# Value products in four 64x64 quarters of the array, keys in chunks of 64 per head, and a new plan, in an attention and token-mixing kernel

## The chip, the cores and the metric

The kernel runs on one core of one Trainium2 chip, in one launch. The metric is the device time of the whole program in microseconds (us). Everything is in 32-bit floats; matrix products of full precision are built on TensorE either from pairs of rounded parts (`float32r`) or from plain `float32` operands.

## The reference, cut to what matters

`q`, `k` and `v` are 8 batches x 8 heads x 576 positions x 64 numbers. The scores are scaled, all scores below the row's maximum minus `tau` are masked, and a softmax follows. The heads of a batch are laid side by side and give `x` (8 x 576 x 512), which goes through a mixture over channels and tokens.

```python
scores = scale * np.matmul(q, k.transpose(0, 1, 3, 2))
thresh = np.max(scores, axis=-1, keepdims=True) - tau
scores = np.where(scores >= thresh, scores, -1000000000.0)
attn = np.exp(scores - np.max(scores, axis=-1, keepdims=True))
attn = attn / (np.sum(attn, axis=-1, keepdims=True) + 1e-09)
x = np.matmul(attn, v)
...
theta = x @ w_theta
y = einsum('ts,bsd->btd', w_tok_r, x * cos(theta)) + einsum('ts,bsd->btd', w_tok_i, x * sin(theta))
u = x + y
out = u + np.maximum(u @ w_ch, 0.0)
```

## The kernel before, in words

The work is cut into 32 pairs of heads (`n`), four to a batch. For each pair, `attention` (L997) loads and splits `q` and `k` (`prepare_q` L500, `prepare_k` L512), loads `v` (`load_v` L520), runs five units, two groups of value products, and a division. After the four pairs of a batch the `mixture` (L758) of that batch follows; its steps are mixed in time with the attention of the next batch.

A **unit** (L535) is a block of 128 queries of both heads (`i` from 0 to 3), or the last 64 queries of both heads in one block (`i` = 4). It has these steps. The score products (L552) go into PSUM banks 0 to 3: for `i` < 4 two products at a time, each on 64 rows of the array (one head each), 12 matmuls of 288 columns. In the first five pairs (`n < AT["pp"]`, with `pp` = 5) VectorE reduces both heads' scores to the negated maximum (L567), ScalarE takes the exponential straight from PSUM (L614), and VectorE masks straight from PSUM and sums (L621). In the other pairs VectorE first copies the negated scores to SBUF and finds the maximum in the same instruction (L583), ScalarE (L631) and VectorE (L638) work from the copy. `nm` holds the thresholds (L592 or L600). TensorE then transposes the weights in blocks of 128x128 (L654, L681), and ScalarE copies them from PSUM into `a0` or `a1` (L660, L668, L686, L694). In the last unit ScalarE first copies 64 columns (L674).

The **value products** (`values`, L698, matmuls at L710) are made twice per pair: group 0 for the first 256 queries, group 1 for the other 320. Each has, for both heads, five chunks of 128 keys; the fifth holds 64 keys of each head, and the other half of its weights are zeros (`v5`). The stationary operand is 128 rows x 64 columns, so one head's product uses the left 64 columns of the array and the other head's the right 64, both into one PSUM bank, one in the upper and one in the lower 64 partitions. Operands are plain `float32`, and the trace shows two MATMUL and two LDWEIGHTS instructions for each product: 20 per group. ScalarE copies the result to `xT` (L717).

`divide` (L721) turns the row sums into reciprocals on VectorE (L734), writes them to DRAM, reads them back spread over the partitions (three DMAs, L737) and multiplies (L745).

`convert` (L377) makes the two `float32r` parts of the 64-bit weights: four chunks of `w_theta` and nine of `w_tok` at the start, four of `w_ch` in the first mixture. Each chunk costs five VectorE instructions (L411, L418, L425, L432, L436), ScalarE instructions (L407, L447, L461) and three products (L455 to L457).

The order on every engine is written by a planner, `Plan.run` (L147): it simulates the five engines with a cost per step and puts first, of the steps that could start within `AT["wait"]` of the earliest, the one with the smallest key. Keys count 9 per pair, plus the offsets in `AT` (L33). `bank()` (L322) gives PSUM banks 7 to 2, or only 7 to 4 for steps of the first pairs. All DMAs go through the SP queue.

Of the kernel before, what the change touches and what calls it, by code (L numbers as in the profile page):

```python
# [32 lines left out]
AT = {  # L33
    "wait": 0.046, "margin": 0.0, "held": 1.639, "theta": 3.43, "theta_by": 2.2, "tok": 17.5, "tok_by": 0.87, "ch": 54.39,
    "ch_by": 3.55, "q": -4.49, "k": -10.75, "raw": -1.58, "v": -4.5, "m0": 8.15, "m1": 4.1, "score": -2.04, "nm": 0.6,
    "add": -4.86, "exp": -2.35, "mask": -0.34, "wrap": -0.65, "turn": 0.32, "copy": 1.0, "last": 0.06, "v0": 4.11, "v1": 13.27,
    "vcopy": -0.32, "div": 6.28, "rows": -1.77, "dmul": 0.16, "x": 0.95, "x_by": 0.51, "wm": -9.49, "ev": 2.19, "zst": 0.37,
    "sin": -0.88, "zm": -0.69, "zh": 0.09, "zl": -2.61, "y": -0.99, "u": 1.64, "fa": 0.68, "fa_by": 1.07, "ft": 0.17,
    "ft_by": 0.05, "pq": 28, "px": 2, "pu": 0, "pz": 6, "pk": 1, "ta": 4, "cut": 2, "pp": 5, "vm": 0, "m6": 0.15, "wp": 0,
    "wq": 0, "ua": 2, "ord": 0, "hang": 0, "n_rawq": 2, "n_rawk": 2, "n_q": 4, "n_rb": 2, "n_ang": 2, "n_xh": 4, "n_xl": 4,  # L40
    "n_wm": 3, "n_z": 3, "n_k": 4, "n_s2": 3, "n_nm": 4, "n_sc": 4, "n_a0": 1, "n_a1": 1, "n_zh4": 4, "n_zl4": 4, "n_zh1": 2,
    "n_zl1": 2, "n_xT": 7, "n_v": 2, "n_rows": 2, "n_rt": 1, "keep": -3.37,
}

# [62 lines left out]
class Plan:  # L107
# [39 lines left out]
    def run(self):  # L147
# [51 lines left out]
        while todo:  # L199
# [50 lines left out]
def tile_attn_moe(  # L250
# [13 lines left out]
    S = S - 64  # L264
# [40 lines left out]
    v5_t = []  # L305
    for i in range(3):
        v5 = const.tile([P, 2, D], F32, name=f"v5{i}")
        nc.gpsimd.memset(v5, 0.0)
        v5_t.append(v5)

# [11 lines left out]
    def bank(early=False):  # L322
        return Buf(cl["bank"], lambda i: psum[:, i], psum=True, places=(7, 6, 5, 4) if early else (7, 6, 5, 4, 3, 2))
# [9 lines left out]
    def c_ps(n):  # L333
        return n / 960 + 0.085

    def c_two(n):
        return n / 960 + 0.14

    def c_fast(n):
        return n / 1920 + 0.05  # L340
# [4 lines left out]
    def c_pool(n):  # L345
        return n * 0.0024 + 0.02
# [32 lines left out]
    v5_b = [fixed(x) for x in v5_t]  # L379

    def convert(src, n, raw_cls, places, key, done, turn):
# [21 lines left out]
        def bb():  # L403
# [3 lines left out]
            c_act(n), lambda: nc.scalar.activation(out=mb().bitcast(F32), in_=hb().bitcast(F32), func=AF.Abs), key, (raw,), (mag,)  # L407
        )
        dve(
            c_fast(n),  # L410
            lambda: nc.vector.tensor_scalar(  # L411
                out=mb().bitcast(F32), in0=mb().bitcast(F32), scalar1=W_LEAST, scalar2=W_MOST, op0=ALU.max, op1=ALU.min
            ),
            key, (mag,), (mag,), lock=True,
        )
# [17 lines left out]
            key, (bits,), (mag,), lock=True,  # L433
# [15 lines left out]
        for c in range(0, n, n2):  # L449
            ps = bank(AT["pp"] and key < PER)  # L450
# [61 lines left out]
    def prepare_k(n, key):  # L512
        pr = pairs[n]
        raw = sb("rawk", [P, QS])
        load(lambda: nc.sync.dma_start(raw(), kT[n // NP, n % NP]), key + AT["raw"], (), (raw,), 320)
        k1, k2 = pr.k = [sb("k", [P, QS], F32R) for _ in range(2)]
        act(c_act(QS), lambda: nc.scalar.copy(out=k1(), in_=raw()), key, (raw,), (k1,))
        low(ON_POOL("k", n, 0), lambda: k2(), lambda: raw(), lambda: k1().bitcast(F32), key, (raw, k1), (k2, 0), QS)

    def load_v(n, key):  # L520
        pr = pairs[n]
        pr.v, pr.v5 = sb("v", [P, 8, D]), v5_b[n % 3]

        def issue():
            nc.sync.dma_start(pr.v(), vp[n // NP, n % NP, :, :8])
            for j in range(2):
                r = slice(64 * j, 64 * j + 64)
                nc.sync.dma_start(pr.v5()[r, j], vp[n // NP, n % NP, r, 8])

        load(issue, key, (), (pr.v, pr.v5), 300, 3)  # L530
# [4 lines left out]
    def unit(n, i):  # L535
# [3 lines left out]
        s, nm = sb("s2", [P, 2, S]), sb("nm", [P, 4])  # L539
# [6 lines left out]
        def score():  # L546
            for x, (a, c) in enumerate(terms):
                for h in range(2):
                    for j in heads:
                        k0 = h * HS + (64 if j == 0 else 0)  # L550
                        r = slice(64 * j, 64 * j + 64) if i < 4 else slice(0, P)
                        nc.tensor.matmul(  # L552
                            ps()[:, 2 * j + h, :HS], q[a]()[r, i * P : (i + 1) * P], k[c]()[r, k0 : k0 + HS], start=(x == 0), stop=(x == 2)
# [7 lines left out]
        def view(ap):  # L561
            return ap.rearrange("p (a b) -> p a b", a=2)

        if n < AT["pp"]:
            dve(
                c_ps(S * len(heads)),
                lambda: nc.vector.tensor_reduce(  # L567
                    out=nm()[:, : len(heads)], in_=ps()[:, :, :HS].rearrange("p (j h) k -> p j h k", h=2),
# [518 lines left out]
```

## Time and profile before

| what | us |
|---|---|
| runs of the kernel | 1036.29, 1034.57, 1035.54 |
| median of these | 1035.54 |
| the profiled execution, its own time | 1035.99 |
| its span, first to last instruction | 1034.2 |
| TensorE matmul (PE) busy | 995.1 |
| VectorE (DVE) busy | 797.8 |
| ScalarE (ACT) busy | 690.8 |
| GpSimd (POOL) busy | 233.8 |

A line such as "L710 PE MATMUL out<-in 128\*64 128x320 f32 x640 | 96.4, 449 | 2.4" gives the source line, the engine, the operation, the tiles written and read, for TensorE the rows\*columns of the array that are used, the shape of the moving operand, the count, the busy time in us, the mean duration of one in ns, and the idle time of the engine just before. Matmuls overlap one another, so the duration of one is longer than its share of the engine's time; the time that a group takes is read from the start of the group to the start of the next. PEld is the loading of stationary operands.

### The profile page before, as it was taken

The numbers are of one execution on the slowest core, as the hardware profiler recorded it, in microseconds if no ns is written. First come the engines' busy times: TensorE is split into PE (matmuls) and PEld (weight loads), VectorE is DVE, ScalarE is ACT, GpSimd is POOL, SyncE is SP. The second block draws the span as 40 slices with busy tenths as digits, with TensorE's granted clock in tenths as the row PEclk, the third lists the DMA queues.
The fourth block names the chain that finished last, engine by engine and source line by source line (L and its number), as shares of the span: only waits on it lengthen the run. The fifth ranks groups of instructions, "written<-read, shape, count | busy, mean of one in ns | idle before, by whom it ended". The sixth has DMA issues, their size and how long they took to land.

```text
span 1034.2 us, 21024 instructions
## 1 busy us (share of the span) xinstructions
PE 995.1 (96%) x8008; PEld 853.7 (83%) x8008; DVE 797.8 (77%) x1869; ACT 690.8 (67%) x1326; POOL 233.8 (23%) x257
## 2 busy tenths in 40 slices
PE   5888889999999999999999999999999999999998
PEld 3566578789898888898888888988888898888998
DVE  6998569987868778777877777887787869887462
ACT  6878577756786468765787558775687647864350
POOL 1002133111261123411252023511242112100100
PEclk9999899999999999999999999999999999999999
DMA  7651132234421143213430152212431142200601
GB/s 254 204 193 50 49 107 73 82 132 134 123 90 46 51 142 110 71 39 112 134 106 26 40 166 92 88 50 70 137 126 37 45 138 97 65 15 13 189 30 67
DMA packets 52308, 98.04 MB, mean 95 GB/s; under 512 B 12752, under 2 KB 21488, under 8 KB 52208
## 3 DMA queue, kind: packets, MB, share of 16 engines
q1 hardware_dynamic: 52208, 96.71, 29.1%
q8 instruction: 63, 1.03, 0.4%
q14 instruction: 37, 0.30, 0.1%
HBM read 82.90 MB, written 13.78 MB: 93 GB/s over the span
## 4 chain that ended last, share of the span: by engine, by line
PE 87%; DVE 6%; ACT 5%; issue 1%; DMA 1%; SPq 0%; ACTq 0%; DVEq 0%
PE banks_ps__66 L932 21%; PE banks_ps__66 L791 19%; PE banks_ps__66 L710 16%; PE banks_ps__66 L552 14%; PE banks_ps__66 L654 12%; PE banks_ps__66 L903 2%; PE banks_ps__66 L681 1%; DVE s L621 1%; DVE nm L567 1%; PE banks_ps__66 L455 1%; ACT a L660 1%; DVE zl L912 1%; DVE sc L583 1%; DMA z<-in_w_tok_dram 1%; PE banks_ps__66 L726 1%
## 5 line engine op out<-in xcount | busy, mean ns | idle before, releaser
L631 ACT ACTIVATE s<-sc,nm 128x576 f32<-128x576 f32 x243 | 186.5, 780 | 83.7 <-DVE sc L583 83.0
L638 DVE SCALAR_TENSOR_TENSOR s<-sc,nm,s 128x576 f32<-128x576 f32 x243 | 204.5, 869 | 39.0 <-ACT s L631 31.6
L583 DVE TENSOR_SCALAR_CACHE_REDUCE sc<-banks_ps__66 128x576 f32<-128x576 f32 x243 | 177.5, 746 | 66.2 <-PE banks_ps__66 L552 65.8
L660 ACT COPY a<-banks_ps__66 128x512 f32<-128x512 f32 x256 | 150.2, 591 | 94.0 <-PE banks_ps__66 L654 92.9
L654 PE MATMUL banks_ps__66<-ident,s 128*128 128x128 f32 x1152 | 173.4, 279 | 13.8 <-DVE s L621 12.9
L552 PE MATMUL banks_ps__66<-k,q 64*128 64x288 f32 (+1 forms) x1728 | 170.2, 311 | 7.7 <-ACT q L509 7.7
L710 PE MATMUL banks_ps__66<-a,v 128*64 128x320 f32 (+1 forms) x1280 | 171.8, 417 | 2.9 <-ACT a L668 1.7
L791 PE MATMUL banks_ps__66<-xh,wm 128*128 128x288 f32 x1024 | 171.6, 302 | 0.0
L932 PE MATMUL banks_ps__66<-wt_h,zh 128*128 128x288 f32 x576 | 166.1, 309 | 1.8 <-DVE zl L912 1.5
L654 PEld LDWEIGHTS banks_ps__66<-ident,s 128*128 128x128 f32 x1152 | 134.5, 142 | 40.2 <-DVE s L621 16.3
L368 POOL TENSOR_TENSOR k<-rawk,k 128x320 fp32r<-128x320 f32 x64 | 60.8, 972 | 460.5 <-issue 255.1
L932 PE MATMUL banks_ps__66<-wt_l,zh 128*128 128x288 f32 x576 | 162.4, 302 | 0.0
L552 PEld LDWEIGHTS banks_ps__66<-k,q 64*128 64x128 f32 (+1 forms) x1728 | 135.1, 188 | 32.0 <-issue 19.6
L791 PEld LDWEIGHTS banks_ps__66<-xh,wm 128*128 128x128 f32 x1024 | 144.8, 189 | 3.2 <-issue 2.2
L710 PEld LDWEIGHTS banks_ps__66<-a,v 128*64 128x64 f32 x1280 | 89.0, 139 | 67.4 <-issue 11.1
L932 PEld LDWEIGHTS banks_ps__66<-wt_h,zh 128*128 128x128 f32 x576 | 108.4, 188 | 4.9 <-DVE zl L912 3.2
L932 PEld LDWEIGHTS banks_ps__66<-wt_l,zh 128*128 128x128 f32 x576 | 108.6, 189 | 0.5 <-issue 0.5
L878 POOL TENSOR_TENSOR z<-z,xT 128x288 f32<-128x288 f32 x96 | 83.0, 905 | 94.5 <-ACT z L859 94.5
L791 PE MATMUL banks_ps__66<-xl,wm 128*128 128x288 f32 x512 | 98.3, 307 | 0.0
L932 PE MATMUL banks_ps__66<-wt_h,zl 128*128 128x288 f32 x576 | 97.5, 301 | 0.0
L932 PEld LDWEIGHTS banks_ps__66<-wt_h,zl 128*128 128x128 f32 x576 | 81.8, 188 | 2.2 <-issue 1.6
L791 PEld LDWEIGHTS banks_ps__66<-xl,wm 128*128 128x128 f32 x512 | 75.0, 189 | 2.0 <-issue 2.0
(79 smaller groups left out, 1249.3 us busy)
## 6 DMA issues: line engine op xcount, KB each, us to landing
wm<-wm_dram SPq DMA_DIRECT2D x64, 512.0 KB, 3.1
rawk<-in_kT_dram SPq DMA_DIRECT2D x32, 320.0 KB, 2.9
rawq<-in_qT_dram SPq DMA_DIRECT2D x32, 320.0 KB, 2.9
out_dram<-xT SPq DMA_DIRECT2D x31, 288.0 KB, 4.0
v<-in_vp_dram SPq DMA_DIRECT2D x32, 256.0 KB, 2.6
z<-in_w_tok_dram SPq DMA_DIRECT2D x9, 576.0 KB, 4.7
rb<-sums_dram SPq DMA_DIRECT2D x32, 144.0 KB, 3.1
wm_dram<-rb SPq DMA_DIRECT2D x16, 256.0 KB, 2.9
```

The source lines that it names most:

```text
L368: eng.tensor_tensor(out=out()[:, c0:c1], in0=in0()[:, c0:c1], in1=in1()[:, c0:c1], op=ALU.subtract)
L552: nc.tensor.matmul(ps()[:, 2 * j + h, :HS], q[a]()[r, i * P : (i + 1) * P], k[c]()[r, k0 : k0 + HS], start=(x == 0), stop=(x == 2))
L583: lambda j=j, sv=sv, sc=sc: nc.vector.tensor_scalar(out=view(sc()), in0=sv(), scalar1=-1.0, scalar2=None, op0=ALU.mult, op1=ALU.min, accum ...
L631: lambda j=j, sc=sc: nc.scalar.activation(out=s()[:, j], in_=sc(), func=AF.Exp, bias=nm()[:, j : j + 1], scale=-1.0),
L638: lambda j=j, sc=sc, total=total: nc.vector.scalar_tensor_tensor(out=s()[:, j], in0=sc(), scalar=nm()[:, 2 + j : 3 + j], in1=s()[:, j], op ...
L654: nc.tensor.transpose(out=tp()[:, c * P : (c + 1) * P], in_=s()[:, j, k0 : k0 + P], identity=ident)
L660: lambda j=j, tp=tp: nc.scalar.copy(out=a()[:, j:8:2, q0 : q0 + P], in_=tp().rearrange("p (c q) -> p c q", c=4)),
L710: nc.tensor.matmul(o()[64 * j : 64 * j + 64, :w], st, mv, start=(c == 0), stop=(c == 4))
L791: nc.tensor.matmul(ps[h]()[:, :HS], wm()[:, a, c, :], parts[c][bb]()[:, h * HS : (h + 1) * HS], start=first and n == 0, stop=final and n = ...
L878: eng.tensor_tensor(out=zi, in0=zi, in1=x[m]()[:, c0:c1], op=ALU.mult)
L903: nc.tensor.transpose(out=tp()[:, i * P : (i + 1) * P], in_=z()[:, c : c + P], identity=ident)
L932: nc.tensor.matmul(ps()[:, :HS], zz[c][lo]()[:, zz[c][2]], w[:, c, hs], start=(q + n == 0), stop=(q + n == len(work) - 1),)
```

## The change

Value products: the weights of both heads are kept side by side, 64 keys of head 0 and 64 keys of head 1 in each 128 columns (`s2` is now 128 x 9 x 2 x 64), and in the odd query blocks the two heads change places. So one transpose brings 64 keys of both heads, and the upper 64 partitions of `a` hold head 0 for the even and head 1 for the odd query block. `v` is loaded twice, once into each half of the partitions. A value product is then 64 rows x 64 columns: for each of 9 chunks four products, one for each quarter of the array, of 128 columns in group 0 and 160 in group 1, into two banks, one per parity of the query block. In each bank one product comes from the upper rows and one from the lower rows, into different halves of the partitions. The zero half of the fifth chunk is gone. With two instructions per product, a group has 72 MATMUL and 72 LDWEIGHTS.

Copies: a result has two copies in group 0 and four in group 1; the last unit's transposes have six copies of 64 partitions instead of two and two small ones, and its copy of 64 columns is gone. `v` has two DMAs of 288 KB instead of three smaller ones, the spreading of the reciprocals four instead of three; `k` has 576 columns instead of 640. `n_rawk` goes from 2 to 1.

Softmax: the variant with the copied scores is used for all pairs. Conversions: the first VectorE instruction (L411) becomes two GpSimd instructions for the 13 chunks at the start. Plan: all offsets are new, the costs of steps are new, a change of array shape has a cost by kind, steps that keep the shape are favoured, and `bank()` always has banks 7 to 2. The score products, the transposes' number and size, and the mixture's products are as before.

```diff
-    "wait": 0.046, ... "theta": 3.43, "theta_by": 2.2, "tok": 17.5, "tok_by": 0.87, ...
+    "wait": 0.053, ... "theta": 1.36, "theta_by": 2.66, "tok": 10.13, "tok_by": 3.87, ...
-    ... "pp": 5, ... "n_rawk": 2, ...
+    ... "n_rawk": 1, ... "linger": 0.03, "v_r": -0.13, "v_m": 0.0, "t_s": -0.57, "m_s": 2.38, "wc": 13,
+def SWITCH(old, new):
+    if old is None or (old in "mt" and new in "mt") or old == new:
+        return 0.0
+    if new == "t":
+        return 0.15
+    if old in "rv" and new in "rv":
+        return 0.145 if new == "v" else 0.196
+    return 0.198
...
+        def favour(o):
+            if o.mode == "v":
+                return AT["v_r"] if mode == "r" else AT["v_m"]
+            if mode not in ("r", "v") or o.mode == mode:
+                return 0.0
+            return AT["t_s"] if o.mode == "t" else AT["m_s"]
...
-            t0 = min(t for t, _ in got) + AT["wait"]
+            t0 = min(t for t, _ in got)
+            if e == PE:
+                t0 += AT["linger"]
+                return min(((o.key + favour(o), o.n), t, o) for t, o in got if t <= t0)[1:]
+            t0 += AT["wait"]
...
-                form = o.mode if o.mode in "vr" else "m"
-                if mode is not None and mode != form:
-                    occ += 0.1
-                mode = form
+                occ += SWITCH(mode, o.mode)
+                mode = o.mode
...
+        if turn < AT["wc"]:
+            for i in range(2):
+                gps(
+                    c_pool(n // 2), lambda i=i: clamp(nc.gpsimd, slice(n * i // 2, n * (i + 1) // 2)), key, ((mag, i),),
+                    ((mag, i),),
+                )
+        else:
+            dve(c_fast(n), lambda: clamp(nc.vector), key, (mag,), ((mag, [0, 1]),), lock=True)
...
-    def values(parts, key):
-        outs = [bank(n < AT["pp"]) for n, _ in parts]
+    def values(n, g, key):
+        pr, x = pairs[n], xT[n]
+        w, a, v = (P, P + 32)[g], pr.a[g], pr.v
+        outs = [bank(), bank()]
         def products():
...
-                for c in range(5):
-                    for j in range(2):
-                        st = pr.v()[:, 4 * j + c, :] if c < 4 else pr.v5()[:, j, :]
-                        mv = a()[:, 2 * c + j] if c < 4 else a()[:, 8]
-                        nc.tensor.matmul(o()[64 * j : 64 * j + 64, :w], st, mv, start=(c == 0), stop=(c == 4))
+            for c in range(9):
+                for par in range(2):
+                    for r in range(2):
+                        h = r ^ par
+                        rows, cols = slice(64 * r, 64 * r + 64), slice(64 * h, 64 * h + 64)
+                        nc.tensor.matmul(
+                            outs[par]()[cols, :w], v()[rows, c, h, :], a()[rows, c, par, :w], start=(c == 0), stop=(c == 8)
+                        )
```

## Rows read from the trace of the kernel before

**Rows 1.** The page, busy time of the engines.

```profile
PE 995.1 (96%) x8008; PEld 853.7 (83%) x8008; DVE 797.8 (77%) x1869; ACT 690.8 (67%) x1326; POOL 233.8 (23%) x257
```

**Rows 2.** Busy time by stretch: PE, PEld, DVE, ACT, POOL, clock, DMA.

```profile
0.00:28.00 28.00, 15.49 (x102) 10.81 (x102) 18.55 (x41) 18.52 (x31) 4.50 (x13) 1.00 0.71 251
28.00:58.00 30.00, 25.39 (x174) 17.37 (x173) 29.64 (x61) 26.74 (x55) 2.42 (x2) 1.00 0.70 226
...
88.00:118.00 30.00, 23.12 (x177) 17.55 (x175) 20.88 (x41) 21.03 (x43) 8.28 (x10) 0.94 0.15 43
...
185.00:960.00 775.00, 774.40 (x6413) 673.14 (x6412) 612.58 (x1500) 531.72 (x1024) 193.91 (x204) 1.00 0.28 87
```

**Rows 3.** The page, chain that ended last, by line.

```profile
PE banks_ps__66 L932 21%; PE banks_ps__66 L791 19%; PE banks_ps__66 L710 16%; PE banks_ps__66 L552 14%; PE banks_ps__66 L654 12%; PE banks_ps__66 L903 2%; PE banks_ps__66 L681 1%; DVE s L621 1%; DVE nm L567 1%; PE banks_ps__66 L455 1%; ACT a L660 1%; DVE zl L912 1%; DVE sc L583 1%; DMA z<-in_w_tok_dram 1%; PE banks_ps__66 L726 1%
```

**Rows 4.** Chain in order of time: start, us, what; value groups.

```profile
402.05 5.00 PE banks_ps__66 L710 x40
...
465.62 2.84 PE banks_ps__66 L710 x20
...
479.81 2.31 PE banks_ps__66 L710 x20
```

**Rows 5.** Timeline of PE near 430 us: start, us, what.

```profile
429.42 1.06 PE L552 MATMUL banks_ps__66<-k,q 64*128 64x288 f32 x12
430.41 2.91 PE L710 MATMUL banks_ps__66<-a,v 128*64 128x320 f32 x20
433.25 1.09 PE L654 MATMUL banks_ps__66<-ident,s 128*128 128x128 f32 x8
434.18 0.27 PE L681 MATMUL banks_ps__66<-ident,s 128*128 128x128 f32 x1
```

**Rows 6.** Groups by line, whole span, weight loads and transposes.

```profile
L654 PE MATMUL banks_ps__66<-ident,s 128*128 128x128 f32 x1152 | 173.4, 279 | 13.8 <-DVE s L621 12.9 <-DVE s L638 0.9
...
L654 PEld LDWEIGHTS banks_ps__66<-ident,s 128*128 128x128 f32 x1152 | 134.5, 142 | 40.2 <-DVE s L621 16.3 <-issue 11.7 <-DVE nm L600 4.8
...
L710 PEld LDWEIGHTS banks_ps__66<-a,v 128*64 128x64 f32 x1280 | 89.0, 139 | 67.4 <-issue 11.1 <-ACT a L668 2.6 <-ACT a L660 1.6
```

**Rows 7.** Groups by line, whole span, softmax on VectorE.

```profile
L638 DVE SCALAR_TENSOR_TENSOR s<-sc,nm,s 128x576 f32<-128x576 f32 x243 | 204.5, 869 | 39.0 <-ACT s L631 31.6 <-ACT a L660 0.5
...
L583 DVE TENSOR_SCALAR_CACHE_REDUCE sc<-banks_ps__66 128x576 f32<-128x576 f32 x243 | 177.5, 746 | 66.2 <-PE banks_ps__66 L552 65.8
...
L621 DVE SCALAR_TENSOR_TENSOR s<-banks_ps__66,nm,s 128x576 f32<-128x576 f32 x45 | 35.2, 813 | 5.2 <-ACT s L614 4.7
...
L567 DVE TENSOR_REDUCE nm<-banks_ps__66 128x2 f32<-128x1152 f32 x20 | 26.8, 1340 | 14.0 <-PE banks_ps__66 L552 13.9
...
L638 DVE DVE_READ_ACCUMULATOR s<-sc,nm,s 128x1 f32 x243 | 19.2, 79 | 0.0
...
L592 DVE TENSOR_SCALAR nm<-nm,small 128x2 f32<-128x2 f32 x20 | 5.0, 249 | 0.3
```

**Rows 8.** Groups by line, VectorE, first 118 us.

```profile
L567 DVE TENSOR_REDUCE nm<-banks_ps__66 128x2 f32<-128x1152 f32 x16 | 21.4, 1340 | 8.2 <-PE banks_ps__66 L552 8.1
L425 DVE SCALAR_TENSOR_TENSOR xh<-z,xh 128x576 uint32<-128x576 uint32 x9 | 7.3, 806 | 0.0
...
L411 DVE TENSOR_SCALAR xl<-xl 128x576 f32<-128x576 f32 x9 | 4.0, 447 | 0.0
...
L411 DVE TENSOR_SCALAR xl<-xl 128x512 f32<-128x512 f32 x4 | 1.7, 418 | 0.0
```

**Rows 9.** Groups by line, whole span, copies on ScalarE.

```profile
L668 ACT COPY a<-banks_ps__66 128x512 f32<-128x512 f32 x32 | 18.8, 588 | 13.6 <-PE banks_ps__66 L654 13.3
...
L717 ACT COPY xT<-banks_ps__66 128x320 f32<-128x320 f32 x32 | 13.7, 429 | 27.0 <-PE banks_ps__66 L710 27.0
L694 ACT COPY a<-banks_ps__66 64x64 f32<-64x64 f32 x64 | 13.0, 204 | 0.4
```

**Rows 10.** Groups by line, whole span, GpSimd's longest instructions.

```profile
L368 POOL TENSOR_TENSOR q<-rawq,q 128x320 fp32r<-128x320 f32 x56 | 61.2, 1115 | 1.3 <-POOL k L368 1.1 <-ACT q L509 0.2
```

More of the change, by code (lines that the diff above doesn't have):

```diff
@@ L33 @@
 AT = {
[L34 to L42, printed above, removed]
-}
+    "wait": 0.053, "margin": 0.0, "held": 1.155, "theta": 1.36, "theta_by": 2.66, "tok": 10.13, "tok_by": 3.87, "ch": 43.55,
@@ L449, in convert @@
         for c in range(0, n, n2):
-            ps = bank(AT["pp"] and key < PER)
+            ps = bank()
             def sum_up(c=c, ps=ps):
@@ L559, in unit, with flat @@
         )
[L561 to L568, printed above, removed]
-                    axis=mybir.AxisListType.XY, op=ALU.max, negate=True,
-                ),
-                t0 + AT["nm"], ((ps, list(heads)),), ((nm, list(heads)),),
-            )
+        def flat():
+            return s().rearrange("p c h k -> p (c h k)")
@@ L684, in unit @@
-        if i < 4:
-            act(
-                c_act(P, True), lambda: nc.scalar.copy(out=a()[:, 8, q0 : q0 + P], in_=t5()[:, :P]), t0 + 1 + AT["last"],
-                (t5,), ((a, (i, 5)),),
-            )
-        else:
-            def last():
-                for jj in range(2):
-                    r = slice(64 * jj, 64 * jj + 64)
-                    nc.scalar.copy(out=a()[r, 8, 256:320], in_=t5()[r, r])
-            act(2 * c_act(64, True), last, t0 + AT["last"], (t5,), ((a, (i, 5)),))
@@ new lines, in unit, with keys, weights @@
+        for j in heads:
+            sc, total = scs[j], i + 5 * j
+            def keys(ap):
+                return ap.rearrange("p (c k) -> p c k", k=D)
+            def weights(j=j):
+                return s()[:, :, j ^ (i % 2), :] if i < 4 else keys(flat()[:, :S])
+            act(
+                c_act(S, ptr=True),
+                lambda j=j, sc=sc, weights=weights: nc.scalar.activation(
+                    out=weights(), in_=keys(sc()), func=AF.Exp, bias=nm()[:, j : j + 1], scale=-1.0
+                ),
+                t0 + j + AT["exp"], (sc, (nm, j)), ((s, j),),
+            )
+            dve(
+                c_two(S) + 0.077,
+                lambda j=j, sc=sc, total=total, weights=weights: nc.vector.scalar_tensor_tensor(
+                    out=weights(), in0=keys(sc()), scalar=nm()[:, 2 + j : 3 + j], in1=weights(), op0=ALU.is_le, op1=ALU.mult,
+                    accum_out=pr.rows()[:, total : total + 1],
+                ),
+                t0 + j + AT["mask"], (sc, (nm, 2), (s, j)), ((s, j), (pr.rows, total)), lock=True,
+            )
@@ L723, in divide @@
         rows, x = pr.rows, xT[n]
-        tp, rt, rc, kept = bank(n < AT["pp"]), sb("rt", [9, P]), sb("rb", [P, S]), fixed(sums_dram[n])
+        tp, rt, rc, kept = bank(), sb("rt", [9, P]), sb("rb", [P, S]), fixed(sums_dram[n])
         pe(
@@ L1008, in attention @@
                 unit(n, i)
[L1009 to L1014 removed]
+            values(n, 0, t + AT["v0"])
+            values(n, 1, t + AT["v1"])
+            divide(n, t + AT["div"])
     for n in range(B * NP):
```

273 lines of the change are left out of this document (105 added, 168 removed).

## The prediction

> **What bounds the kernel now.** I read the page's busy line first: the matmul rows of TensorE fill 96% of the span, VectorE 77%, ScalarE 67% [rows 1]. Such a share says little alone, so the view by stretches comes next. It shows two regimes [rows 2]. From 185 to 960 us TensorE has a matmul running for 774.4 of 775 us at the full clock (1.00, the 2.4 GHz level), while VectorE is at 79% and ScalarE at 69%: there only TensorE's own time counts. Before that the four pairs of the first batch have no mixture beside them; from 28 to 58 us VectorE is busy 29.6 of 30 us and TensorE has gaps, so there VectorE's time counts. The chain of waits agrees: its large shares are products, the value products (L710) 16% of the span, and the softmax of the first pairs (L621, L567) stands in it with 1% each [rows 3].
>
> How dear is a value group? In the chain a group of 256 queries stands with 2.31 us, one of 320 with 2.84 us, and one of each back to back with 5.00 us [rows 4]. So the pair together saves 0.15 us: that is what changing the array's shape costs a group. It leaves 2.16 and 2.69 us for ten rounds each (20 matmuls, two side by side, one in each column half): 0.216 and 0.269 us per round, 0.00083 us per column and almost nothing fixed. Serial, 20 matmuls would take twice that.
>
> **The change, step by step,** against the profiled execution (1035.99 us; span 1034.2 us). The median of the runs is 1035.54 us, 0.45 us lower. About 0.2% (2.1 us) is what a measurement can tell from no change.
>
> Value products. A group now has 72 matmuls, 18 for each quarter. If four quarters run side by side, that is 18 rounds of 128 or 160 columns: by the row of 256, less 0.00083 us per column, 0.110 and 0.1365 us. 18 rounds give 1.98 and 2.46 us, in place of 2.16 and 2.69 us; the 0.15 us stays. The gain is the zero half of the fifth chunk, 0.18 and 0.23 us. Counted in the chain, 26 groups of the first kind and 27 of the second start behind 185 us: 26 x 0.18 + 27 x 0.23 = **-10.9 us**. The other groups lie where TensorE waits for VectorE; I count nothing for them (all of them would be 2.2 us more). No row shows four quarters at once. The score products show two row halves side by side (12 matmuls of 288 columns from 429.42 to 430.41 us, 0.165 us for two, the shape change included) [rows 5], the value products two column halves; I take four, because both halvings are seen to work alone. The other end, two at a time, is the first rival.
>
> Changes of shape. The planner now prices them at up to 0.2 us and puts steps of the same shape first. What one is worth is the 0.15 us above. Counted in the timeline between 200 and 960 us, 45 of 101 runs of score products are followed by a full-array product and 27 by a value group (the first row of the timeline's extract is one of these) [rows 5]; each further joining saves some 0.15 us. There are 12 value runs that follow something else: 12 x 0.15 = **-2 us**. Ends: 0, as the old plan already joins most, and -5 (also every other score run left more cheaply).
>
> The first 118 us, by VectorE. A unit of two heads pays now one reduction (1.340), the threshold (0.249) and two masks with their sums (0.813 + 0.08 each): 3.38 us. With copied scores it pays two copies (0.746 + 0.079), the threshold and two masks (0.869 + 0.079): 3.80 us [rows 7]. That is +0.42 us for each of four units and about +0.15 us for the last, +1.85 us per pair and +7.4 us for four. The clamps that go to GpSimd take away 9 x 0.447 + 4 x 0.418 = 5.7 us [rows 8]. The chunks of the token weights are now spread 3.87 keys apart from 10.13 on, so that two of nine (37.2 and 41.1) come behind the fourth pair, which ends at 36; their four remaining instructions, of 0.45 to 0.81 us each [rows 8], I estimate at 2.5 us together: -5 us. Sum: -3.3 us. The copied scores also free PSUM before the exponential, so that the next score products need not wait for the masks; VectorE waited 8.1 us for them here [rows 8]. I take **-4 us**; ends -11 (all of that wait gone) and +8 (the dearer softmax, no relief).
>
> GpSimd gets 26 half clamps. Its own rows for about that size are two-operand ones, up to 1.115 us [rows 10]; 26 of these are 29 us, in a stretch in which it is busy 4.5 of 28 and 2.4 of 30 us [rows 2]. Behind a clamp in its queue are the splits of the next pair's `q` and `k`, and score products wait for them. These are prepared a unit or more ahead, so I count 0; without that cover two clamps, 2 us per chunk.
>
> ScalarE. Copies of 64 and of 512 columns take 0.204 and 0.588 us [rows 9], so one of 256 some 0.37 us and one of 128 some 0.26 us. The last unit's six copies cost 4 x 0.37 + 2 x 0.204 = 1.9 us against 1.0 us, the results' copies about 1.45 us against 0.80 us (0.429 us for the wide one [rows 9], some 0.37 us for the other). That is 1.5 us per pair, 40 us for 27 pairs: 572 of 775 us, 74%. TensorE hides it with the mixture's products, so 0; uncovered, +40 us.
>
> DMAs. `v` grows by some 290 KB per pair; at the 226 to 251 GB/s of the start that is 1.3 us per pair, with the DMA engines already 0.70 busy there [rows 2]. The four descriptors for the spreading and two for `v` instead of three and three leave SP's queue as long as it was; behind them stand the loads of the next `q` and `k`, which are asked for ahead. `n_rawk` 1 makes a load of `k` wait for the split of the last one, within a pair's time. I count 0; ends 0 and +5 us (four pairs at the start). The two banks per value group, instead of one, are drawn from six; 0, for the same cover as ScalarE's.
>
> Sum: 1035.99 - 10.9 - 2 - 4 = **1019.1 us**; I say 1019.0.
>
> **Rivals.** *Quarters two at a time* (slower). The quarters of one parity write the same bank from different row halves. The score products' two row halves go to different banks [rows 5], and the value products' two halves that share a bank use all rows, so no row shows what the new pattern does. If the second had to wait for the first, there would be 36 rounds: 36 x 0.110 + 0.15 = 4.11 us against 2.31, and 36 x 0.1365 + 0.15 = 5.06 us against 2.84: +1.80 and +2.22 us, 107 us in all, and with the other terms 1137 us. It decides as soon as two such quarters cannot start in the same round. Against it: the halves of the partitions are different, as for the two column halves now. The Trainium skill, page TensorEngine Tiling, section Gotcha 1: PSUM Pressure, says that different row tiles write to different banks and cannot use one bank simultaneously; taken literally, that is this rival. Chance 0.08.
>
> *The queue is too slow* (slower). The densest that rows show is 12 matmuls with their weight loads in 0.99 us [rows 5], 0.0825 us for each; 72 at that pace take 5.9 us, and 6.1 us with the change of shape, against 2.31 and 2.84 us: 186 us in all, 1216 us. That row is set by the array, so it bounds from above only; a pace under 0.0275 us, which the forecast needs for 18 rounds in 1.98 us, stands in no row. The Trainium skill, page TensorE: Matmul & The Clock Gate, section Wait — 56ns, not 53.3ns?, names 62 ns per MATMUL when the sequencer decodes in software; by it a group would take 4.6 us, an estimate of 108 us in all. Chance 0.04.
>
> *The weight load shows* (no change). A load of 64 columns lasts 0.139 us [rows 6], longer than a round of 0.110 us. If it could not overlap, both groups would take 18 x 0.139 = 2.50 us: +0.34 and -0.19 us, +4 us in all, and 1034 us with the other gains. Against it: transposes load for 0.142 us each [rows 6] and yet eight of them run from 433.25 to 434.18 us [rows 5], one every 0.116 us. Chance 0.07.
>
> *TensorE waits in the middle.* ScalarE's 40 us or a clumsier order of the new plan gives gaps behind 185 us that were not there: anything from 1030 to 1060 us. For it: the plan is new throughout. Against it: ScalarE has 26% left. Chance 0.04.
>
> **The numbers.** The forecast has 0.77, its own range being 1008 (-10.9, -5, -11, and the groups at the start) to 1030 us (-10.9, 0, and half of the +8 and +5 taken). The weight load's 1034 us belongs in the range, and the mild part of the waiting: 1008 to 1038 us. Left out are the two slow rivals (0.12) and some 0.06 at both ends. Faster: 0.77 and 0.02 of the weight load; same: 0.04 of it and 0.02 of the waiting; slower: the two slow rivals, 0.01 and 0.02: 0.79, 0.06 and 0.15.
>
> **What would show it.** Right: a group of 72 matmuls takes about 2.1 or 2.6 us from its start to the next step; the period of a batch falls by some 1.7 us, four pairs' worth; TensorE still without gaps in the middle; the first batch's last pair done some 4 us earlier. Wrong: groups of 4 us or more (two at a time, or the queue), groups alike at 2.65 us (weight loads), or idle time of PE behind ScalarE's copies.

## The result, and the profile after

The changed kernel takes 1012.12 us (median of 4 runs, 1011.27 to 1013.10) against 1035.91 us for the kernel before (4 runs, 1034.57 to 1036.68): 0.9772 of its time [0.9755, 0.9789]. That is -23.8 us where -17 was forecast, inside the range; the two largest terms of the sum were both off, in opposite directions, and that the time still fell into the range is in part luck. The profiled execution took 1011.61 us, its span 1009.8 us (-24.4).

The page's busy line of the changed kernel, which answers to [rows 1]:

```profile
PE 980.6 (97%) x11336; PEld 904.0 (90%) x11336; DVE 787.3 (78%) x1921; ACT 719.3 (71%) x1518; POOL 267.8 (27%) x280
```

The view by stretches (PE, PEld, DVE, ACT, POOL, clock, DMA), of the kernel before for the first 185 us:

```profile
118.00:150.00 32.00, 29.63 (x221) 23.61 (x221) 21.74 (x42) 19.56 (x40) 4.69 (x7) 0.89 0.29 95
...
0.00:185.00 185.00, 151.32 (x1076) 113.35 (x1077) 149.26 (x303) 135.97 (x263) 36.29 (x49) 0.95 0.39 130
```

and of the changed kernel:

```profile
88.00:118.00 30.00, 27.59 (x350) 23.07 (x351) 29.86 (x76) 26.72 (x65) 9.39 (x9) 0.94 0.37 98
118.00:150.00 32.00, 31.13 (x391) 28.58 (x382) 30.07 (x71) 29.15 (x63) 13.32 (x14) 1.00 0.32 98
...
0.00:185.00 185.00, 165.16 (x1909) 138.72 (x1910) 169.32 (x412) 159.12 (x338) 78.67 (x76) 0.97 0.51 150
...
185.00:940.00 755.00, 750.60 (x8887) 701.28 (x8885) 583.49 (x1446) 537.39 (x1139) 185.55 (x200) 1.00 0.33 97
```

The span is TensorE's matmul time plus the time in which it has none, so these rows split the -24.4 us. Matmul time fell by 14.5 us (995.1 to 980.6). Time without a matmul fell by 13.9 us in the first 185 us (33.7 to 19.8), rose by 3.8 us in the middle (0.6 us up to 960 [rows 2], 4.4 us up to 940) and by 0.1 us after it. **Over half of the gain lies in the first 185 us, where VectorE now sets the pace**: it did 169.3 us of work there, not 149.3, and from 88 to 118 us it is busy 29.86 of 30 us (20.88 before [rows 2]).

TensorE's clock is a part of this that the forecast did not name. From 118 to 150 us, behind a stretch in which TensorE had a matmul running for 23.1 of 30 us [rows 2], the granted clock was 0.89 in the kernel before, so some of it ran at the lower level, 1.2 GHz; in the changed kernel it was 1.00 there, behind 27.6 of 30 us. Over the thirteen runs of the kernel before that stand beside the tenth round (below), the span goes with the mean clock, from 1036.2 us at 0.990 to 1028.6 us at 0.998; the four of the changed kernel lie between 1009.4 and 1011.3 us at 0.995 to 0.998, in no such order. How much of the early gain is clock, no run separates.

The ends of the batches (start of the last store of a batch, for batch 7 of the first of the last two, us from the start of the span, read from the timeline of SyncE) show the same:

| end of batch | 0 | 1 | 3 | 5 | 7 |
|---|---|---|---|---|---|
| before | 259.3 | 378.4 | 616.8 | 855.3 | 1029.8 |
| changed | 240.3 | 358.3 | 594.9 | 832.3 | 1005.4 |
| difference | -19.0 | -20.1 | -21.9 | -23.0 | -24.4 |

From batch 0 to batch 5 a batch takes 119.2 us before and 118.4 us after: 0.8 us less, not the 1.7 us that I had announced. Between these two ends TensorE's matmul time fell by 1.5 us per batch (595.4 to 588.1 us for five), and its time without a matmul rose by 0.7 us (0.6 to 3.9 us for five).

The value groups themselves are what was forecast. The chain of waits of the changed kernel (start, us, what) has for one group of each kind and for a pair:

```profile
698.22 2.12 PE banks_ps__66 L669 x72
700.34 0.59 PE banks_ps__66 L634 x4
...
714.02 4.57 PE banks_ps__66 L669 x144
...
773.27 2.61 PE banks_ps__66 L669 x72
```

2.12, 2.61 and 4.57 us stand where 2.31, 2.84 and 5.00 us stood [rows 4].

The softmax of the first pairs, groups by line, VectorE, first 118 us (answers to [rows 7, 8]):

```profile
L616 DVE SCALAR_TENSOR_TENSOR s<-sc,nm,s 128x576 f32<-128x576 f32 x43 | 35.9, 852 | 0.6 <-ACT s L609 0.4
L586 DVE TENSOR_SCALAR_CACHE_REDUCE sc<-banks_ps__66 128x576 f32<-128x576 f32 x44 | 32.2, 746 | 2.1 <-PE banks_ps__66 L568 2.1
```

44 heads' scores are copied in this stretch; before, 36 heads were reduced there (16 reductions of two heads [rows 8] and 4 of one). The wait for score products fell from 8.1 us to 2.1 us although each head costs more. Over the first 185 us the view of waits (VectorE; us in total, times, longest) has, before and after:

```profile
DVE nm L567 <- PE banks_ps__66 L552: 14.7, 10, 3.7
```

```profile
DVE sc L586 <- PE banks_ps__66 L568: 2.6, 5, 1.0
```

What TensorE waits for in the middle is new. The view of waits, PE, 185 to 940 us (the kernel before has none there):

```profile
PE banks_ps__66 L690 <- ACT xT L678: 2.2, 6, 0.4
PE banks_ps__66 L634 <- ACT a L652: 1.8, 5, 0.4
PE banks_ps__66 L634 <- ACT a L640: 0.3, 1, 0.3
```

and one of them in the timelines of ScalarE and of PE (start, us, what):

```profile
382.82 1.28 ACT L824 ACT_TABLE_LOAD   x1
384.11 0.78 ACT L827 ACTIVATE z<-z,small 128x576 f32<-128x576 f32 x1
...
386.72 1.28 ACT L831 ACT_TABLE_LOAD   x1
388.02 0.78 ACT L609 ACTIVATE s<-sc,nm 128x576 f32<-128x576 f32 x1
...
389.74 0.60 ACT L678 COPY xT<-banks_ps__66 128x128 f32<-128x128 f32 x3
```

```profile
383.59 4.64 PE L669 MATMUL banks_ps__66<-a,v 64*64 64x128 f32 x144
...
390.30 0.27 PE L690 MATMUL banks_ps__66<-ident,rows 128*9 128x128 f32 x1 [0.42 <-ACT xT L678]
```

ScalarE is in its block of sines with a table load before and behind it while the value products run (383.6 to 388.2 us); their results, now in four banks instead of two, are copied only from 389.74 us on, and TensorE stands 0.42 us for one of these banks. The same wait comes in each of the six batches of this stretch.

### The profile page after: what moved, and what is told of

Read it like the earlier page. It is cut to its first block, busy times and chain, and to the rows that moved or that the text cites. A ratio compares the mean times of both kernels' runs of the same rounds, so it can differ in the third digit from the quotient of the medians.

```text
span 1009.8 us, 27890 instructions
## 1 busy us (share of the span) xinstructions
PE 980.6 (97%) x11336; PEld 904.0 (90%) x11336; DVE 787.3 (78%) x1921; ACT 719.3 (71%) x1518; POOL 267.8 (27%) x280
## 5 line engine op out<-in xcount | busy, mean ns | idle before, releaser
L616 DVE SCALAR_TENSOR_TENSOR s<-sc,nm,s 128x576 f32<-128x576 f32 x288 | 245.0, 873 | 41.1 <-ACT s L609 35.4
L609 ACT ACTIVATE s<-sc,nm 128x576 f32<-128x576 f32 x288 | 216.4, 778 | 73.4 <-DVE sc L586 69.9
L586 DVE TENSOR_SCALAR_CACHE_REDUCE sc<-banks_ps__66 128x576 f32<-128x576 f32 x288 | 209.5, 752 | 64.3 <-PE banks_ps__66 L568 64.2
L640 ACT COPY a<-banks_ps__66 128x512 f32<-128x512 f32 (+1 forms) x384 | 169.7, 489 | 74.0 <-PE banks_ps__66 L634 72.4
L634 PE MATMUL banks_ps__66<-ident,s 128*128 128x128 f32 (+1 forms) x1312 | 203.4, 279 | 6.2 <-DVE s L616 2.6
L568 PE MATMUL banks_ps__66<-k,q 64*128 64x288 f32 (+1 forms) x1728 | 174.3, 313 | 10.4 <-ACT q L529 7.7
L634 PEld LDWEIGHTS banks_ps__66<-ident,s 128*128 128x128 f32 (+1 forms) x1312 | 151.7, 141 | 26.3 <-issue 11.2
L568 PEld LDWEIGHTS banks_ps__66<-k,q 64*128 64x128 f32 (+1 forms) x1728 | 137.7, 189 | 34.9 <-issue 16.4
L669 PE MATMUL banks_ps__66<-a,v 64*64 64x128 f32 (+1 forms) x4608 | 153.8, 285 | 0.0
L669 PEld LDWEIGHTS banks_ps__66<-a,v 64*64 64x64 f32 x4608 | 139.5, 133 | 8.7 <-issue 5.6
L381 POOL TENSOR_TENSOR k<-rawk,k 128x288 fp32r<-128x288 f32 x64 | 63.2, 1007 | 257.6 <-ACT k L537 256.0
L381 POOL TENSOR_TENSOR xl<-xT,xh 128x288 fp32r<-128x288 f32 x32 | 26.4, 849 | 225.5 <-ACT xh L720 213.3
```

Of the source, the lines that this page charges most:

```text
L381: eng.tensor_tensor(out=out()[:, c0:c1], in0=in0()[:, c0:c1], in1=in1()[:, c0:c1], op=ALU.subtract)
L568: nc.tensor.matmul(ps()[:, 2 * j + h, :HS], q[a]()[r, i * P : (i + 1) * P], k[c]()[r, h * HS : (h + 1) * HS], start=(x == 0), stop=(x == 2),)
L586: lambda j=j, sc=sc: nc.vector.tensor_scalar(out=sc().rearrange("p (a b) -> p a b", a=2), in0=ps()[:, 2 * j : 2 * j + 2, :HS], scalar1=-1. ...
L609: lambda j=j, sc=sc, weights=weights: nc.scalar.activation(out=weights(), in_=keys(sc()), func=AF.Exp, bias=nm()[:, j : j + 1], scale=-1.0),
L616: lambda j=j, sc=sc, total=total, weights=weights: nc.vector.scalar_tensor_tensor(out=weights(), in0=keys(sc()), scalar=nm()[:, 2 + j : 3 ...
L634: nc.tensor.transpose(out=tp()[: k1 - k0, c * P : (c + 1) * P], in_=flat()[:, k0:k1], identity=ident)
```

## The experiments

The theory when they were made: TensorE's own saving in the value groups sets the gain behind 185 us, and the early gain comes from the first batch's softmax and conversions on VectorE. The rivals: it is the new plan alone (offsets and shape rules), or the clamps on GpSimd, or each early part by itself. Where an edit leaves the planner free, it also writes another order, and so do the three edits of the kernel before, which come first; "orders kept" means that every engine's steps stand in the changed kernel's order.

**Copied scores alone, in the kernel before.** `pp` = 0 also gives the other steps of the first pairs banks 7 to 2 instead of 7 to 4.

```diff
-    "ft_by": 0.05, "pq": 28, "px": 2, "pu": 0, "pz": 6, "pk": 1, "ta": 4, "cut": 2, "pp": 5, "vm": 0, "m6": 0.15, "wp": 0,
+    "ft_by": 0.05, "pq": 28, "px": 2, "pu": 0, "pz": 6, "pk": 1, "ta": 4, "cut": 2, "pp": 0, "vm": 0, "m6": 0.15, "wp": 0,
```

> The kernel before with copied scores in the first five pairs too (pp = 0), nothing else. The changed kernel is 18 us ahead by the end of the first mixture. Theory A, the copied scores bring most of that (PSUM free before the masks, VectorE no longer waiting 8 us for score products): 8 to 14 us faster than before, 1022 to 1028 us. Rival B, they are only dearer on VectorE (+0.42 us per unit) and the conversions brought the gain: no faster, 1034 to 1043 us.

Measured: 1037.47 us against 1035.51, 1.0019 [1.0008, 1.0029]. The first batch ends 3.1 us earlier, the second 2.1 us later. Alone it gains nothing, although VectorE's wait for score products in the first 185 us falls to 3.7 us (14.7 before).

**Conversions spread alone, in the kernel before.**

```diff
-    "wait": 0.046, "margin": 0.0, "held": 1.639, "theta": 3.43, "theta_by": 2.2, "tok": 17.5, "tok_by": 0.87, "ch": 54.39,
+    "wait": 0.046, "margin": 0.0, "held": 1.639, "theta": 1.36, "theta_by": 2.66, "tok": 10.13, "tok_by": 3.87, "ch": 54.39,
```

> The kernel before with only the times at which the conversions are due taken from the change (spread over four and a half pairs). Theory D, VectorE ran out of filling work after 90 us in the kernel before: the first mixture ends 3 to 8 us earlier, 1027 to 1033 us. Rival: score products hold VectorE up anyway (14.7 us): no change, 1034 to 1038 us.

Measured: 1034.93 us, 0.9997 [0.9982, 1.0013]; the first batch ends 0.4 us earlier. VectorE still waits 12.8 us for score products in the first 185 us (14.7 before).

**Both of these, in the kernel before.** The edits are the two above together.

> The kernel before with copied scores in the first five pairs and with the changed due times of the conversions. Alone they ended the first mixture 3.1 us and 0.4 us earlier. If the two need one another (VectorE free to run ahead, and work to fill it): the first mixture ends 8 us earlier or more. If the early gain needs the whole new plan: 2 to 5 us earlier, and 1033 to 1039 us in all.

Measured: 1023.40 us against 1035.42, 0.9891 [0.9869, 0.9914]: -12.0 us, where the two apart give +2.0 and 0. The first 185 us by stretch, first copied scores alone, then spreading alone, then both:

```profile
0.00:185.00 185.00, 153.34 (x1077) 118.99 (x1077) 155.86 (x371) 136.51 (x262) 40.11 (x49) 0.94 0.41 132
```

```profile
0.00:185.00 185.00, 149.89 (x1079) 112.73 (x1080) 149.08 (x305) 136.23 (x264) 36.13 (x49) 0.96 0.40 130
```

```profile
0.00:185.00 185.00, 163.95 (x1164) 125.64 (x1165) 163.43 (x389) 143.69 (x280) 44.75 (x53) 0.97 0.43 139
```

With both, VectorE's work in it (third busy time) rises from 149.3 to 163.4 us; with copied scores alone, whose instructions are dearer, it is 155.9 us. TensorE's time without a matmul falls from 33.7 to 21.1 us (31.7 and 35.1 us with one of them). The difference lies late in the stretch: from 88 to 150 us VectorE is busy 42.6 of 62 us before, 44.2 with copied scores, 40.8 with the spreading, 55.5 with both. With copied scores alone VectorE waits in one place 6.6 us for the reciprocals to come back from DRAM and 4.7 us for ScalarE's angles; with the spreading alone it waits for score products. From batch 1 to batch 5 the period is 119.1 us. So half of the gain can be had without the quarters, together with the order that the planner wrote for these two edits; a kept order has not priced it. The profiled execution was the slowest of four (1026.47 us, mean clock 0.995; the others, of 1022.3 to 1023.4 us, had 1.00): in it the first batch ends 11.6 us earlier and the last 9.5 us.

**A tenth round in every value group, orders kept.** It puts back two rounds per group, about what the quarters saved: chunk 0 is multiplied twice, the first time only to be overwritten.

```diff
-            for c in range(9):
+            for x, c in enumerate((0, *range(9))):
...
-                            outs[par]()[cols, :w], v()[rows, c, h, :], a()[rows, c, par, :w], start=(c == 0), stop=(c == 8)
+                            outs[par]()[cols, :w], v()[rows, c, h, :], a()[rows, c, par, :w], start=(x < 2), stop=(x in (0, 9))
```

> The changed kernel, order of all engines as it is, with a tenth round of four quarter products in each value group (the first chunk once more, overwritten). It puts back the tensor time that the change took away: two rounds of 0.110 and 0.1365 us per group, 0.49 us per pair. If the middle is bound by TensorE and the quarters gave their time one for one: 53 groups, 12 to 14 us slower than the changed kernel, 1024 to 1027 us. Rival, the tensor time saved mostly became waiting for ScalarE's copies: under 6 us slower, 1012 to 1018 us.

Measured: 1021.36 us, 0.9886 [0.9840, 0.9932]. Against the changed kernel's orders on the same chip (the next experiment, 1012.26 us) that is +9.1 us. Its chain and its waits of PE from 185 to 945 us:

```profile
50.84 2.34 PE banks_ps__66 L669 x80
...
165.61 2.88 PE banks_ps__66 L669 x80
```

```profile
PE banks_ps__66 L634 <- ACT a L652: 1.8, 5, 0.4
PE banks_ps__66 L634 <- ACT a L640: 0.2, 1, 0.2
```

Each group is longer by 0.22 or 0.27 us; over the 53 groups behind 185 us counted as in the forecast, that is 26 x 0.22 + 27 x 0.27 = 13.0 us, but only 9.1 us come out at the end (8.2 us by the spans of the two profiled executions, 1018.4 and 1010.2 us). With four runs of each, one of them 5 us above its fellows, this is known to a few us; the ends of the batches show it more sharply. From batch 0 to batch 5 a batch takes 119.8 us here and 118.3 us in the next experiment: 1.5 us more, where the longer groups make 4 x 0.22 + 4 x 0.27 = 2.0 us. The first batch ends no later (240.3 us, 241.4 us in the next experiment): there the length of the groups costs nothing. The waits for L678, the copies of value results, are gone, and TensorE's time without a matmul falls by 2.4 us in the middle (busy times as above, 185 to 940 us, the next experiment first, then this one):

```profile
185.00:940.00 755.00, 750.49 (x8892) 701.62 (x8890) 583.05 (x1447) 538.00 (x1141) 186.43 (x200) 1.00 0.33 97
```

```profile
185.00:940.00 755.00, 752.89 (x9158) 704.96 (x9158) 583.26 (x1441) 536.34 (x1130) 180.39 (x200) 1.00 0.33 95
```

**A quarter to 30% of what the shorter groups save comes back as TensorE's waiting for copies of value results.** The waits for L652 and L640, the copies of the transposed weights, stay.

**The clamps issued on VectorE, orders kept.** VectorE does a whole clamp where GpSimd did two halves.

```diff
-                    c_pool(n // 2), lambda i=i: clamp(nc.gpsimd, slice(n * i // 2, n * (i + 1) // 2)), key, ((mag, i),),
+                    c_pool(n // 2), lambda i=i: clamp(nc.vector) if i == 0 else None, key, ((mag, i),),
```

> The changed kernel with the clamps issued on VectorE at the places where GpSimd had them, all other orders kept. Theory C, the 28 us of the free plan with clamps on VectorE came from the planner falling into another order and not from the clamps: 1014 to 1020 us (5.7 us of VectorE at the start). Rival: the clamps' engine matters by itself: 1030 us or more.

Measured: 1012.26 us, 0.978 [0.9747, 0.9812], the changed kernel's time. The first batch ends 1.1 us later, the last 0.4 us. The clamps' place is worth nothing that can be measured.

**The clamps on VectorE, planner free.**

```diff
-    "v_r": -0.13, "v_m": 0.0, "t_s": -0.57, "m_s": 2.38, "wc": 13,
+    "v_r": -0.13, "v_m": 0.0, "t_s": -0.57, "m_s": 2.38, "wc": 0,
```

> The changed kernel with all clamps back on VectorE. If VectorE's time sets the first 118 us, its 5.7 us come back: 1015 to 1018 us. If the clamps lie beside a VectorE that has slack, or GpSimd's port costs VectorE as much: 1010 to 1014 us.

Measured: 1039.95 us, 1.0044 [1.0027, 1.0061], 28 us above the changed kernel. The order kept shows that this is the order, not the clamps: from 185 to 940 us TensorE waits 14.0 us where the kernel with the same clamps and the order kept does not.

```profile
PE banks_ps__66 L759 <- DVE zl L880: 14.0, 5, 2.8
```

**Softmax from PSUM in the first five pairs, planner free.** The steps of the kernel before come back for these pairs.

```diff
-    "fa_by": 1.32, "ft": 0.17, "ft_by": 0.05, "pq": 28, "px": 2, "pu": 0, "pz": 6, "pk": 1, "ta": 4, "cut": 2, "pp": 0,
+    "fa_by": 1.32, "ft": 0.17, "ft_by": 0.05, "pq": 28, "px": 2, "pu": 0, "pz": 6, "pk": 1, "ta": 4, "cut": 2, "pp": 5,
...
+        def early():
...
+                lambda: nc.vector.tensor_reduce(
+                    out=nm()[:, : len(heads)], in_=ps()[:, :, :HS].rearrange("p (j h) k -> p j h k", h=2),
+                    axis=mybir.AxisListType.XY, op=ALU.max, negate=True,
...
```

> The changed kernel with the first five pairs' softmax straight from PSUM again, all else as changed (banks 7 to 2 for all). Theory A, copied scores bring the gain at the start: 1019 to 1026 us. Rival B, they cost VectorE 7 to 9 us there and other things brought the gain: 1003 to 1013 us.

Measured: 1043.94 us, 1.0087 [1.0066, 1.0109]. The first batch ends 33.7 us later than in the changed kernel, and from there on the distance stays (33.2 us at the end). In the first 185 us TensorE waits for the masks. The transposes (L680, L736) read what the masks write; only the 7.0 us of the score products (L568) are a wait for PSUM that the masks still read:

```profile
PE banks_ps__66 L680 <- DVE s L617: 7.0, 5, 3.9
PE banks_ps__66 L568 <- DVE s L617: 7.0, 6, 3.3
PE banks_ps__66 L736 <- DVE s L617: 5.2, 4, 2.0
```

**No shape rules.**

```diff
-    "v_r": -0.13, "v_m": 0.0, "t_s": -0.57, "m_s": 2.38, "wc": 13,
+    "v_r": 0.0, "v_m": 0.0, "t_s": 0.0, "m_s": 0.0, "wc": 13,
...
-    return 0.198
+    return 0.1
```

> The changed kernel with a change of shape priced at 0.1 us whatever its kind, as before, and no step favoured for its shape; all offsets as changed. My sum gave these rules 2 us: 1012 to 1016 us if the order stays as good otherwise. Theory E in another form, any free edit puts the plan off its tuned order: 1020 us or more, with other groups of steps following one another in the middle.

Measured: 1028.84 us, 0.9944 [0.9927, 0.9961], 17 us above the changed kernel, 6.9 of them at the end of the first batch, about 2 per batch after it.

**The old offsets in the changed kernel.** All due times are those of before, the prices and rules the new ones.

```diff
-    "wait": 0.053, "margin": 0.0, "held": 1.155, "theta": 1.36, "theta_by": 2.66, "tok": 10.13, "tok_by": 3.87, "ch": 43.55,
+    "wait": 0.046, "margin": 0.0, "held": 1.639, "theta": 3.43, "theta_by": 2.2, "tok": 17.5, "tok_by": 0.87, "ch": 54.39,
...
```

> The changed kernel with the offsets of the plan before; the new costs, the prices of shape changes, the rules on keeping a shape and the clamps on GpSimd stay. Beside the run with the whole old plan (1081 us) it differs by costs, rules and clamps; beside the changed kernel by offsets alone. Theory E, the offsets made for these steps carry most of the plan's share: 1045 us or more. Rival, the truer costs and the shape rules carry it: 1012 to 1025 us.

Measured: 1066.04 us, 1.0301 [1.0282, 1.0320].

**The whole old plan in the changed kernel.** Offsets, costs of steps, prices, rules and the clamps are those of before (`n_rawk` stays 1 and `bank()` stays as changed), so what is left of the change is mainly the quarters with their copies and loads, and the copied scores.

```diff
-    "n_zh1": 2, "n_zl1": 2, "n_xT": 7, "n_v": 2, "n_rows": 2, "n_rt": 1, "keep": -3.77, "linger": 0.03,
-    "v_r": -0.13, "v_m": 0.0, "t_s": -0.57, "m_s": 2.38, "wc": 13,
+    "n_zl1": 2, "n_xT": 7, "n_v": 2, "n_rows": 2, "n_rt": 1, "keep": -3.37, "turn_by": 0.5, "wc": 0,
...
-                occ += SWITCH(mode, o.mode)
+                if mode is not None and mode != form:
+                    occ += 0.1
```

> The changed kernel's value products, layout and copied softmax under the old planner, old costs and old offsets, clamps on VectorE. Beside the kernel before with copied scores it differs by the value products and their copies alone. If the quarters are worth their 0.42 us per pair whatever the plan: 9 to 13 us below that kernel. Rival: ScalarE's extra copies and the second bank eat it in a plan that was not made for them: less than 5 us below it, or above it, with TensorE waiting for ScalarE in the middle.

Measured: 1081.14 us, 1.0439 [1.0407, 1.0471]: slower than before, though every value group is shorter. From 185 to 1010 us TensorE waits for ScalarE's copies of the weights:

```profile
PE banks_ps__66 L749 <- ACT a L630: 18.1, 6, 3.5
```

The five with the planner free cost 17 to 69 us against the changed kernel each. They fit due times that are good for one set of steps and no other, which is argued from these five and not shown; they don't price the step that was edited.

**Each value product in two of half the columns, orders kept.** 144 MATMUL of 64 or 80 columns per group, the same work for the array.

```diff
-            for c in range(9):
-                for par in range(2):
+            for x0 in (0, w // 2):
+                for c in range(9):
+                    for par in range(2):
```

> The changed kernel, orders kept, with each value product cut into two of half the columns, one half of the group after the other: 144 matmuls and loads per group of 64 and 80 columns, the same columns in sum. If rounds go by columns alone (53 and 67 ns): about 18 x 2.4 ns more per group, 1014 to 1017 us. If a load of weights (0.133 us by its row) or the queue binds below some 0.1 us per round of four: groups of 3.5 us or more in place of 2.1 and 2.6 us, 1060 us or more.

Measured: 1052.95 us, 1.0176 [1.0140, 1.0211]. The chain has a lone group of each kind, the timeline a pair:

```profile
169.88 2.65 PE banks_ps__66 L670 x144
...
183.21 2.26 PE banks_ps__66 L670 x144
```

```profile
397.60 3.76 PE L670 MATMUL banks_ps__66<-a,v 64*64 64x64 f32 x225
402.45 1.33 PE L670 MATMUL banks_ps__66<-a,v 64*64 64x80 f32 x63 [1.09 <-issue]
403.72 0.66 PE L872 MATMUL banks_ps__66<-ident,z 128*128 128x128 f32 x4
```

A lone group takes 2.26 or 2.65 us, against 2.12 and 2.61 with half as many instructions: 2.26 / 144 = 0.0157 us per MATMUL with its weight load, the change of shape included. This pair takes 403.72 - 397.60 = 6.1 us instead of 4.57, with TensorE idle and no releaser in the trace; the others of the trace take 5.7 to 8.7 us. Neither range of the expectation holds: lone groups go by their columns, and yet the time is 41 us longer. The groups by line, whole span:

```profile
L670 PEld LDWEIGHTS banks_ps__66<-a,v 64*64 64x64 f32 x9216 | 156.0, 134 | 42.3 <-issue 38.5 <-ACT a L652 1.4 <-DVE xT L949 0.9
L670 PE MATMUL banks_ps__66<-a,v 64*64 64x80 f32 x4608 | 94.6, 232 | 28.4 <-issue 27.1 <-ACT a L652 0.9
```

Weight loads of 134 ns per MATMUL of 0.0157 us are hidden, so the weight load is no bound. Of the "issue" time before a value matmul, 27.1 us stand before the 80-column ones, all but some 3 us of it in the second group of a pair.

## Why the prediction was right, and where not

**Value products, -10.9 us: the groups right, the worth too large.** 18 rounds and the change of shape gave 2.13 and 2.61 us on paper and 2.12 and 2.61 us in the chain. Over all 64 groups that is 32 x 0.19 + 32 x 0.23 = 13.4 us, against 14.5 us by which TensorE's matmul time fell. The step that failed is "TensorE hides it with the mixture's products, so 0" for ScalarE's copies. ScalarE's busy time rose by 28.5 us in all (690.8 to 719.3), 0.9 us per pair and not 1.5, in part because the sum left out the copy of 64 columns that goes (8.3 us before, L674). (Of the wide copies that the six of the last unit replace there was one per pair, not two: L668 x32 [rows 9].) But the 29% that ScalarE has left is not left where the value copies come due, behind its sines. By the tenth round the saving is worth 9.1 / 13.0 = 0.7 of its size here, an estimate of -7.6 us. The time without a matmul in the middle, 4.4 us in place of 0.6, has two parts of about 2 us each: the waits for L678, which the tenth round takes away, and those for L652 and L640, which it does not. The second come on top, so that some -5.5 us are left of this term, an estimate again, and the table of the ends of batches agrees: behind the first batch the whole change gains 5.4 us (from -19.0 to -24.4), where the terms of value products and of shapes make -12.9. The rival "TensorE waits in the middle" thus happened in small, inside the gain. The Trainium skill, page TensorEngine Tiling, section PSUM Bottleneck, warns that tiling speeds up TensorE and not the emptying of PSUM, so that the copies may bind next. The trace agrees, to 2.2 us of waits for L678.

**Changes of shape, -2 us: not there.** The term supposed more joined runs. Counted in the timeline of TensorE between the ends of batch 0 and batch 5 (transposes taken as full-array steps), the array changes its shape 195 times in the kernel before and 195 times in the changed one, 39 per batch. Nor does matmul time show the gain: per batch it fell by 1.5 us, and the shorter groups alone make 1.7 us. That the plan without these rules is 17 us slower is a matter of its whole order, which no kept order could take apart.

**The first 118 us, -4 us (ends -11 and +8): the term that was mis-sized.** The first batch ends 19.0 us earlier, beyond the term's end of -11. Two of the three edits to which I gave it, copied scores and spread conversions, end it 11.6 us earlier in the kernel before, and gain 12.0 us in all by the medians. The sum added up VectorE's instructions, +7.4, -5.7 and -5, and took next to nothing for the wait of 8.1 us that the same paragraph named. The -5.7 us for the clamps was worth nothing: with the clamps on VectorE and the order kept the kernel takes 1012.26 us. The stretch was too short as well: VectorE stood idle for 35.7 us of the first 185 us before and for 15.7 us after. I had put the dearer softmax first, as work; what counted was VectorE's idle time. Its wait for score products fell from 14.7 to 2.6 us, but this alone is not the cause: copied scores alone bring it to 3.7 us and gain nothing, because VectorE then stands elsewhere. Only with conversions at hand as well is it busy behind 88 us. That the two pay only together I did not see at all.

That the copies help because they free PSUM sooner, as the prediction has it, is argued and not shown. In the kernel before the view of waits has no matmul of a score product behind a mask in the first 185 us; TensorE stands at the transposes, for the masks whose weights they read (the kernel before, then the changed one):

```profile
PE banks_ps__66 L654 <- DVE s L621: 12.9, 9, 3.2
```

```profile
PE banks_ps__66 L634 <- DVE s L616: 2.6, 4, 1.1
```

The remaining part, from -11.6 to -19.0 us at the end of the first batch, comes with the rest of the change. The length of the value groups and the clamps are not it, since the tenth round and the clamps on VectorE, both with orders kept, move that end by 1.1 us at most. As every free planner run writes another order, I could not split the rest. It stays open.

**Right by luck in part.** Where the sum had -4 us for the start and -12.9 us behind it, the ends of the batches have -19.0 and -5.4. Of the four signs of being right, only the times of the groups came: the period fell by 0.8 us and not 1.7, TensorE got gaps in the middle, and the first batch was done 19 us earlier and not 4.

**Counted at 0.** GpSimd's 26 half clamps cost nothing that shows (1012.12 us with them, 1012.26 without). The DMAs: the view of waits of TensorE names none, neither in the first 185 us nor from there to 940 us; the waits of ScalarE and VectorE for DMAs in the first 185 us add up to 11.2 us, 7.9 before, and what these 3.3 us are worth no run shows.

**The rivals that fell.** *Quarters two at a time* needed groups of 4.11 and 5.06 us; they take 2.12 and 2.61. The sentence of the Trainium skill, page TensorEngine Tiling, section Gotcha 1: PSUM Pressure, that different row tiles cannot use one bank simultaneously, is not borne out for this pattern, in which upper and lower rows write one bank in different halves of the partitions. *The queue is too slow* needed over 0.0275 us per MATMUL; 0.0157 us is seen in lone groups. *The weight load shows* needed 2.50 us for both groups alike.

## What to carry to other kernels

Where an engine off the main bound sets the pace for a while (here VectorE in the first batch), price the change by that engine's idle time and by what ends it, not by the sum of its instructions: two edits that are worth nothing apart were worth 12 us together, with the order that the planner made for them. A group on the main bound may be forecast to the hundredth of a microsecond from its rounds, and still a quarter or more of the saving can go back to the engine that empties its results. In a kernel whose order is planned with tuned due times, undo a part with the order kept; a planner left free answers with its own tens of microseconds.

## What was not expected of the hardware

Behind a dense group TensorE can stand with nothing in the trace to wait for. 144 MATMUL of 64 columns with their 144 weight loads ran in 2.26 us alone; in the group directly behind one TensorE stood for "issue", some 24 us in all over the kernel, and pairs took 5.7 to 8.7 us instead of about 4.9. Pairs of 72-MATMUL groups (4.57 us) do not show it. That its instructions ran out is a guess; what supplies them and how far ahead was not measured.

A clamp is much dearer on GpSimd than on VectorE. Groups by line of the changed kernel, whole span:

```profile
L424 POOL TENSOR_SCALAR xl<-xl 128x288 f32<-128x288 f32 x18 | 25.1, 1411 | 38.3 <-ACT xl L419 22.8 <-issue 9.6 <-DVE s L616 5.9
L424 POOL TENSOR_SCALAR xl<-xl 128x256 f32<-128x256 f32 x8 | 9.0, 1146 | 7.7 <-ACT xl L419 7.7
```

Half a chunk takes 1.41 us there, where the whole chunk of 576 columns took 0.447 us on VectorE [rows 8]. GpSimd had the room for these 34 us, so it cost nothing.
